# A GEGLU block with Strassen products: T3 of the second half from DRAM, and M2 of one group next to M1 of the next

## The chip, the cores and the metric

The kernel runs on 1 core of one Trainium2 chip. The metric is device time in microseconds (us), the median of several executions. Before the change it is 539.02 us (three runs, 538.69 to 539.37).

## The reference

```python
"x": (1, 2048, 1024), "w_gate": (1024, 3584), "w_up": (1024, 3584), "w_down": (3584, 1024)  # bf16

def reference(x, w_gate, w_up, w_down):
    return (_gelu(x @ w_gate) * (x @ w_up)) @ w_down     # _gelu: tanh form
```

## The kernel before

The 2048 rows are worked through in two halves (h = 0, 1) of 1024. Each half has two stages. The first computes the hidden values hT = gelu(x @ w_gate) * (x @ w_up), 3584 features by 1024 rows, in bf16 (matmuls at lines 267 and 418). The second, "down", multiplies by w_down in two groups (grp = 0, 1) of 512 rows, one call of `down_group` each (matmuls at line 698). Both stages use a Strassen-Winograd scheme: seven products of half-size blocks in place of eight.

In a down group the blocks are A11, A12, A21, A22 of hT and B11, B12, B21, B22 of w_down. A product has 14 blocks of the contraction (NS = 14) and two row tiles (u = 0, 1), so 28 matmuls of 128x128 by 128x512. M1 = A11 B11 and M2 = A12 B21 read bf16 operands directly. The other five read sums in f32: M5 = S1 T1, M6 = S2 T2, M7 = S3 T3, M3 = S4 B22, M4 = A22 T4. The order is M1, M5, M6, M7, M2, M3, M4. The partial results stay in eight PSUM banks, in four pairs PB, VB, QB, RB: ACT copies M1 from PB to QB, M6 adds to QB, ACT copies that to RB, M7 adds to RB, and so on; M2 adds to PB and closes the first output block.

**The ring of right operands.** T1, T2, T3, B22 (as f32) and T4 of a group, 14 blocks each, pass through a ring `t_mem` of NR = 20 blocks (`right`, line 567). A block's place is its number in that sequence modulo 20. A new pair of blocks can be written when the pair 20 places earlier has been used. `t_down` (line 587) makes one pair: T1 and T3 by a subtraction on DVE (line 600), B22 by a cast on ACT (line 597), T2 and T4 by a 512 KB load from `t_dram` (line 595), where the first stage of h = 0 put them (`stage_step`, line 614, store at line 627). The functions `behind_m5`, `behind_m6`, `behind_m7`, `behind_m3`, `behind_m4` are called after each second block of a product and issue what can go where the used blocks were: T2 and the first of T3 behind M5, T3 behind M6, B22 and the first three pairs of T4 behind M7, the other four pairs of T4 behind M3, the next group's T1 and T2 behind M3 and M4. The left sums S1 to S4 are made on DVE (`s_down`, line 670), A22 is cast on ACT (line 662). The first four blocks of S3 of group one lie in a weight buffer, `early`.

**B21** is loaded by `load_b21` (line 555) behind M6's fifth and sixth block: three tiles of 512 KB from a pool of three buffers (`wd_pool`) and a fourth of 256 KB from the output pool (`o_pool`, four buffers). In group one one of the three buffers is `early`, so the third load waits until M7 has read it.

**Order.** Every engine's queue is fixed by hand: `sp`, `act`, `dve`, `pool` and `pe` chain each instruction behind the last one of its engine, in program order. All loads and stores of the down stage are on SP's one queue. `product` (line 692) takes an order of the matmuls: `plain` goes block by block, both u; `tail` finishes u = 0 five matmuls before the end; `head` begins with five of u = 0.

In group one of h = 0, after M6, `x_fill` (line 997) loads 1 MB of the next half's x from DRAM on SP (line 1000).

Of the kernel before, what the change touches and what calls it, by code (L numbers as in the profile page):

```python
# [11 lines left out]
F32 = mybir.dt.float32  # L12
# [22 lines left out]
def kernel(  # L35
# [8 lines left out]
    nc = tc.nc  # L44
    P = 128
# [8 lines left out]
    NH = 2  # L54
# [4 lines left out]
    DN = 512  # L59
# [9 lines left out]
    NS = KF // 2  # L69
    NR = 20  # L70
    NGRP = SH // TB
# [15 lines left out]
    dram_pool = ctx.enter_context(  # L87
        tc.tile_pool(name="dram", bufs=1, space=bass.MemoryType.DRAM)
    )
# [10 lines left out]
    w_mem = shared_pool.tile([P, 4 * CH + (NS - 4) * DN], BF16, name="w_mem")  # L100
    assert NR * DN == 5 * KH * TB and NS - 4 >= 2 * KD // 2

    t_dram = dram_pool.tile([P, NS, 2, DN], F32, name="t_dram")
    x_dram = dram_pool.tile([KD, P, TB], BF16, name="x_dram")

    banks = [psum.tile([P, TB], F32, name=f"bank{i}") for i in range(8)]
    PB, VB, QB, RB = (0, 1), (2, 3), (4, 5), (6, 7)
    last_on = {}

    def on(engine, inst):  # L110

        if engine in last_on:
            tc.add_manual_dep(
                inst.ins, last_on[engine].ins.name, SCHED_DEP, reason="engine order"
            )
        last_on[engine] = inst
        return inst

    def sp(inst):
        return on("sp", inst)  # L120

    def act(inst):
        return on("act", inst)

    def dve(inst):
        return on("dve", inst)
# [12 lines left out]
    def pe(inst):  # L139
        return on("pe", inst)  # L140
# [391 lines left out]
    def wd_rows(i0, i1):  # L532

        assert i1 <= 8 or i0 >= 8
        e0 = 2 * CH + i0 * D if i1 <= 8 else (i0 - 8) * D
        return w_mem[:, e0 : e0 + (i1 - i0) * D].rearrange("p (a b) -> p a b", b=D)

    def b22_blocks(i0, i1):

        assert i1 <= 4 or i0 >= 4  # L540
        e0 = (NS - 8) * D + i0 * DN if i1 <= 4 else 4 * CH + (i0 - 4) * DN
        return w_mem[:, e0 : e0 + (i1 - i0) * DN].rearrange("p (a b) -> p a b", b=DN)
# [7 lines left out]


    BPT = WDT * D // DN
    b21_tiles = {}

    def load_b21(n, q):
        i0, i1 = q * BPT, min((q + 1) * BPT, NS)
        if i1 < NS:
            w = wd_pool.tile([P, WDT, D], BF16, name="wd_sb")
            w = w[:].rearrange("p a d -> p (a d)")
        else:  # L560
            w = o_pool.tile([P, (i1 - i0) * DN], BF16, name="o_sb")[:]
        w = w.rearrange("p (b n) -> p b n", n=DN)
        src = wdv[:, NS + i0 : NS + i1, 0:DN]
        sp(nc.sync.dma_start(out=w[:, 0 : i1 - i0, :], in_=src))
        b21_tiles[(n, q)] = w

    def right(grp, name, i0, i1):

        r0 = ((grp * len(SEQ) + SEQ.index(name)) * NS + i0) % NR
        assert r0 + i1 - i0 <= NR  # L570
        t = t_mem[:, r0 * DN : (r0 + i1 - i0) * DN]
        return t.rearrange("p (a b) -> p a b", b=DN)
# [14 lines left out]
    def t_down(grp, name, i0, i1):  # L587

        for i in range(i0, i1, 2):
            t = right(grp, name, i, i + 2)  # L590
            rows = wd_rows(i, i + 2)
            b11, b12 = rows[:, :, 0:DN], rows[:, :, DN:D]
            if name in ("t2", "t4"):
                src = t_dram[:, i : i + 2, 0 if name == "t2" else 1, :]
                sp(nc.sync.dma_start(out=t.bitcast(F32), in_=src))
            elif name == "b22":
                act(nc.scalar.copy(out=t, in_=b22_blocks(i, i + 2)))  # L597
            else:
                in0, in1 = (b12, b11) if name == "t1" else (b22_blocks(i, i + 2), b12)
                dve(nc.vector.tensor_tensor(out=t, in0=in0, in1=in1, op=ALU.subtract))  # L600

    staged = {}
# [68 lines left out]
    NSPLIT = 4  # L673
    DH = DN // 2

    def down_group(hT, h, grp, then):
        last_grp = h == NH - 1 and grp == NGRP - 1
        more = grp + 1 < NGRP
        t0 = grp * TB
        n = h * NGRP + grp  # L680

        def done(name):
            for f in then.get(name, ()):
                f()

        plain = [(i, u) for i in range(NS) for u in range(2)]
        tail = [p for p in plain if p[0] < NS - 5]
        tail += [(i, u) for u in range(2) for i in range(NS - 5, NS)]
        head = [(i, u) for u in range(2) for i in range(5)]
        head += [p for p in plain if p[0] >= 5]  # L690

        def product(name, bset, lhs, rhs, start, stop, behind=None, order=plain):

            left_of = [0] * NS
            for i, u, *part in order:
                bank, c0, c1 = part or (bset[u], 0, DN)
                pe(
                    nc.tensor.matmul(  # L698
                        banks[bank][:, c0:c1],
                        lhsT=lhs(i, u),  # L700
                        rhs=rhs(i)[:, c0:c1],
                        start=start and i == 0,
                        stop=stop and i == NS - 1,
                        skip_group_check=True,
                    )
                )
                left_of[i] += 1
                if behind is not None and left_of[i] == 2 and i % 2 == 1:
                    behind(i - 1)

        def h_block(l, j):
            def lhs(i, u):
                c0 = t0 + (2 * l + u) * P
                return hT[:, j * NS + i, c0 : c0 + P]

            return lhs
# [15 lines left out]
        def b21(i):  # L732
            return b21_tiles[(h * NGRP + grp, i // BPT)][:, i % BPT, :]

        def add_m5(dst, src, u):
            dve(
                nc.vector.tensor_tensor(
                    out=banks[dst][:], in0=banks[src][:], in1=m5[u][:], op=ALU.add
                )
            )  # L740

        def evacuate(bset, l, d, halves=False):

            outs = []
            for u in range(2):
                if halves and u == 1:
                    r0 = h * SH + t0 + (2 * l + u) * P
                    for bank, c in ((bset[u], 0), (VB[u], DH)):
                        dst = o_pool.tile([P, DN], BF16, name="o_sb")[:, 0:DH]
                        src = banks[bank][:, c : c + DH]  # L750
                        if c == 0:
                            dve(nc.vector.tensor_copy(out=dst, in_=src))
                        else:
                            act(nc.scalar.copy(out=dst, in_=src))  # L754
                        c0 = d * DN + c
                        outs.append((out2[r0 : r0 + P, c0 : c0 + DH], dst))
                    continue
                dst = o_pool.tile([P, DN], BF16, name="o_sb")[:]
                r0 = h * SH + t0 + (2 * l + u) * P
                if last_grp and u == 0:  # L760
                    dve(nc.vector.tensor_copy(out=dst, in_=banks[bset[u]][:]))
                else:
                    act(nc.scalar.copy(out=dst, in_=banks[bset[u]][:]))  # L763
                outs.append((out2[r0 : r0 + P, d * DN : (d + 1) * DN], dst))
            return outs

        def store(outs):
            for dst, src in outs:
                sp(nc.sync.dma_start(out=dst, in_=src))
# [1 line left out]
        def store_last(dst, src):  # L771
            act(nc.scalar.dma_start(out=dst, in_=src))

        product("m1", PB, h_block(0, 0), b11, True, False)
        for u in range(2):
            act(nc.scalar.copy(out=banks[QB[u]][:], in_=banks[PB[u]][:]))
        done("m1")

        def behind_m5(i):

            s_down(hT, grp, "s2", i, i + 2)
            if NT2 + i < NS:
                t_down(grp, "t2", NT2 + i, NT2 + i + 2)
            elif more:
                late.append(i + NT2 - NS)
            else:
                t_down(grp, "t3", i + NT2 - NS, i + NT2 - NS + 2)
# [12 lines left out]
        def behind_m6(i):  # L800
            if NT2 + i < NS:
                t_down(grp, "t3", NT2 + i, NT2 + i + 2)
            else:
                s_down(hT, grp, "s4", i + NT2 - NS, i + NT2 - NS + 2)
            if i == 4:
                for q in range(4):
                    load_b21(n, q)

        product("m6", QB, lsum(0), rsum("t2"), False, False, behind_m6, tail)
# [1 line left out]
        for u in range(2):  # L811
            act(nc.scalar.copy(out=banks[RB[u]][:], in_=banks[QB[u]][:]))
            add_m5(QB[u], QB[u], u)
        t_down(grp, "b22", 0, NT2)
        done("m6")

# [9 lines left out]
        s_down(hT, grp, "a22", 0, NS)  # L826
        out22 = evacuate(VB, 1, 1)
        done("m7")
        store(out22)
        product("m2", PB, h_block(0, 1), b21, False, True)  # L830
        out11 = evacuate(PB, 0, 0)
        done("m2")


# [6 lines left out]
                    t_down(grp + 1, "t1", NT2 + i - NS, NT2 + i - NS + 2)  # L841

        product("m3", QB, lsum(0), rsum("b22"), False, True, behind_m3)
        store(out11 + evacuate(QB, 0, 1))
        done("m3")

        def behind_m4(i):
            if not more:
# [28 lines left out]
    for h in range(NH):  # L877
# [52 lines left out]
        for lead in range(begin, NPAIR, PPG):  # L930
# [15 lines left out]
            for n, pair in enumerate(members):  # L946
# [7 lines left out]
                if h > 0 and 6 < pair < 11:  # L954
                    i = s3_late[pair - 7]
# [112 lines left out]
```

## Time and profile before

| | |
|---|---|
| median of 3 runs | 539.02 us |
| the profiled execution | 539.16 us |
| its span, first to last instruction | 537.4 us |
| PE (matmul) busy | 533.6 us, 99% |
| DVE, ACT, POOL busy | 367.6, 263.5, 252.2 us |
| DMA, mean over the span | 191 GB/s |
| down stage of h = 0 | 183.0 to 270.9 us |
| down stage of h = 1 | 446.5 to 534.4 us |

Engines: PE is the matmul engine, PEld its weight loads, DVE the vector engine, ACT the scalar engine, POOL GpSimd, SP the queue of SyncE (SPq where it issues a DMA). L595 is line 595 of the kernel. A line of a timeline has the start in us, the length in us, the engine, the line, the operation, what it writes and reads, the number of instructions merged into it and, in brackets, the idle time before it and what ended it. For a DMA on SPq the length is that of the issue; the time to landing is asked for separately. A matmul's recorded length (0.38 to 0.39 us) overlaps the next one's; the distance of the starts is its cost. A line of the chain has start, length, what. A line of a table by stretches has the stretch, its length, each engine's busy time with its number of instructions, the granted PE clock, the DMA engines' share and GB/s. Waits read: who, what it waited for, us in total, times, longest.

### The profile page before, as it was taken

What the parts mean: (1) busy time and instruction counts of PE and PEld (TensorE: products, weight loads), DVE (VectorE), ACT (ScalarE), POOL (GpSimd) and SP (SyncE); (2) the same over time, 40 slices, a digit from 0 to 9 for tenths busy, and PEclk for the clock granted to TensorE, in tenths of its full rate; (3) what the DMA queues carried; (4) which work ended last, traced back from release to release, by engine and by line L of the source; (5) the groups of instructions that cost most, each with busy time, mean ns of one, the idle gap of its engine ahead of it and who ended that gap; (6) DMA issues with size and microseconds to landing.
All of it is one profiled execution on the core that took longest, in us unless ns stands there. A gap on an engine that the chain in (4) does not pass through costs nothing.

```text
span 537.4 us, 7033 instructions
## 1 busy us (share of the span) xinstructions
PE 533.6 (99%) x2388; PEld 379.2 (71%) x2388; DVE 367.6 (68%) x476; ACT 263.5 (49%) x447; POOL 252.2 (47%) x213
## 2 busy tenths in 40 slices
PE   9999999999999999999999999999999999999997
PEld 4568686867677686777768676776768686866866
DVE  2985868787876998989555353444444669979961
ACT  2555555556465329117465554656555551452280
POOL 0698696969696200000056494958677670000000
PEclk9999999999999999999999999999999999999999
DMA  9965759697623887788950413314040329677846
GB/s 220 329 199 134 267 164 304 182 320 199 229 53 143 318 288 243 243 292 292 329 168 12 145 62 97 110 48 154 3 156 22 136 84 337 228 237 250 292 143 212
DMA packets 92547, 102.70 MB, mean 191 GB/s; under 512 B 18656, under 2 KB 67424, under 8 KB 92512
## 3 DMA queue, kind: packets, MB, share of 16 engines
q1 hardware_dynamic: 69568, 80.23, 45.7%
q10 hardware_dynamic: 22944, 22.02, 13.2%
q8 instruction: 19, 0.31, 0.3%
q14 instruction: 16, 0.13, 0.1%
HBM read 85.98 MB, written 12.58 MB: 183 GB/s over the span
## 4 chain that ended last, share of the span: by engine, by line
PE 99%; ACT 0%; issue 0%
PE bank L418 63%; PE bank L698 33%; PE bank L267 3%; PE bank L202 1%; PE bank L311 0%; ACT o_sb L754 0%
## 5 line engine op out<-in xcount | busy, mean ns | idle before, releaser
L418 PE MATMUL bank<-t_mem,s_mem 128*128 128x512 f32 x1056 | 244.6, 392 | 0.0
L418 PEld LDWEIGHTS bank<-t_mem,s_mem 128*128 128x128 f32 x1056 | 198.1, 188 | 42.7 <-issue 0.2
L388 POOL TENSOR_TENSOR s_mem<-w_mem 128x512 fp32r<-128x512 bf16 x102 | 124.0, 1236 | 185.5 <-DMA out_dram<-o_sb 96.9
L698 PE MATMUL bank<-t_mem,s_mem 128*128 128x512 f32 (+1 forms) x548 | 127.2, 391 | 0.0
L698 PEld LDWEIGHTS bank<-t_mem,s_mem 128*128 128x128 f32 x548 | 102.5, 188 | 22.0
L291 DVE TENSOR_TENSOR hT<-w_mem,bank 128x512 bf16<-128x512 f32 x106 | 72.5, 687 | 66.5 <-PE bank L418 44.5
L434 DVE TENSOR_TENSOR bank<-bank,m 128x512 f32<-128x512 f32 x108 | 70.0, 694 | 56.1 <-ACT m L472 54.3
L418 PE MATMUL bank<-xT,w_mem 128*128 128x512 bf16 x432 | 95.7, 379 | 0.0
L286 ACT ACTIVATE w_mem<-bank 128x512 f32<-128x512 f32 x106 | 63.0, 597 | 64.1 <-DVE bank L434 34.8
L418 PEld LDWEIGHTS <-w_mem 128*128 128x128 bf16 x432 | 41.2, 98 | 51.3 <-issue 3.4
L388 POOL TENSOR_TENSOR s_mem<-w_mem,s_mem 128x512 fp32r<-128x512 bf16 x52 | 68.4, 1335 | 2.9 <-PE bank L418 2.9
L600 DVE TENSOR_TENSOR t_mem<-w_mem 128x1024 fp32r<-128x1024 bf16 x56 | 65.9, 1225 | 0.9 <-PE bank L418 0.9
L388 POOL TENSOR_TENSOR s_mem<-s_mem,w_mem 128x512 fp32r<-128x512 f32 x52 | 61.3, 1200 | 0.0
L401 ACT CAST s_mem<-w_mem 128x512 fp32r<-128x512 bf16 x54 | 33.2, 616 | 31.3 <-PE bank L418 30.1
L478 ACT COPY bank<-bank 128x512 f32<-128x512 f32 x54 | 30.8, 570 | 26.6 <-PE bank L418 26.6
L670 DVE TENSOR_TENSOR s_mem<-hT 128x512 fp32r<-128x512 bf16 x52 | 36.7, 745 | 7.1 <-PE bank L698 7.1
L472 ACT COPY m<-bank 128x512 f32<-128x512 f32 x54 | 31.8, 589 | 18.4 <-PE bank L418 18.4
L698 PEld LDWEIGHTS <-hT 128*128 128x128 bf16 x224 | 21.3, 98 | 26.6 <-issue 2.1
L444 ACT COPY bank<-bank 128x512 f32<-128x512 f32 x54 | 30.7, 570 | 14.3 <-PE bank L418 13.5
L625 DVE TENSOR_TENSOR o_sb<-wd_sb,o_sb 128x512 fp32r<-128x512 bf16 x28 | 32.9, 1176 | 0.5
L763 ACT CAST o_sb<-bank 128x512 bf16<-128x512 f32 x27 | 14.8, 585 | 33.8 <-PE bank L698 33.8
L597 ACT CAST t_mem<-w_mem 128x1024 fp32r<-128x1024 bf16 x28 | 26.9, 1047 | 0.0
(46 smaller groups left out, 236.5 us busy)
## 6 DMA issues: line engine op xcount, KB each, us to landing
t_mem<-t_dram SPq DMA_DIRECT2D x56, 512.0 KB, 5.3
w_mem<-in_w_gate_dram ACTq DMA_DIRECT2D x10, 1024.0 KB, 5.4
w_mem<-in_w_up_dram ACTq DMA_DIRECT2D x10, 1024.0 KB, 8.3
wd_sb<-in_w_down_dram SPq DMA_DIRECT2D x28, 256.0 KB, 5.4
t_dram<-o_sb SPq DMA_DIRECT2D x28, 256.0 KB, 3.5
wd_sb<-in_w_down_dram SPq DMA_DIRECT2D x12, 512.0 KB, 7.6
w_mem<-in_w_down_dram SPq DMA_DIRECT2D x4, 1024.0 KB, 6.7
w_mem<-in_w_down_dram SPq DMA_DIRECT2D x8, 512.0 KB, 8.3
```

Of the source, the lines that this page charges most:

```text
L286: act(nc.scalar.activation(out=g_sb, in_=ps[:], func=ACT.Gelu_apprx_tanh))
L291: nc.vector.tensor_tensor(out=hT[:, fc, tb * TB : (tb + 1) * TB], in0=g_sb, in1=ps[:], op=ALU.mult,)
L388: pool(nc.gpsimd.tensor_tensor(out=t, in0=in0, in1=in1, op=op))
L401: act(nc.scalar.copy(out=t, in_=a(1, 1)))
L418: nc.tensor.matmul(banks[bank][:], lhsT=lhs[:, c, :], rhs=rhs[:, c, :], start=start and c == 0, stop=c == KH - 1, skip_group_check=True,)
L434: nc.vector.tensor_tensor(out=banks[dst][:], in0=banks[src][:], in1=m5[:], op=ALU.add)
L472: act(nc.scalar.copy(out=m5[j][:], in_=banks[V_[j]][:]))
L478: act(nc.scalar.copy(out=banks[R_[j]][:], in_=banks[Q_[j]][:]))
L600: dve(nc.vector.tensor_tensor(out=t, in0=in0, in1=in1, op=ALU.subtract))
L625: dve(nc.vector.tensor_tensor(out=t, in0=in0, in1=in1, op=ALU.subtract))
L670: dve(nc.vector.tensor_tensor(out=t, in0=in0, in1=in1, op=op))
L698: nc.tensor.matmul(banks[bank][:, c0:c1], lhsT=lhs(i, u), rhs=rhs(i)[:, c0:c1], start=start and i == 0, stop=stop and i == NS - 1, skip_gr ...
```

## The change

`t_dram` gets a third plane. In group one of h = 0, T3 is still made on DVE; the new `keep_t3`, behind M6, issues seven 512 KB stores of it on SP. In group two of h = 0, T3 is made on DVE as before. In h = 1 (`one_run`) both groups load T3 from there, seven 512 KB loads each, at the places where the subtractions were issued.

In h = 1, M2 leaves its place between M7 and M3. M2 of group one is held and goes in front of group two's M1; group two's M2 follows right behind its M1 (M1 in order `tail`, M2 in order `head`). So the second half runs M1 M5 M6 M7 M3 M4 | M2 M1 M2 | M5 M6 M7 M3 M4. The last group swaps the bank pairs PB and VB. The first three tiles of B21 are loaded once for both groups, behind group one's M6, the fourth twice. In h = 0 the products keep their order.

```diff
-    t_dram = dram_pool.tile([P, NS, 2, DN], F32, name="t_dram")
+    t_dram = dram_pool.tile([P, NS, 3, DN], F32, name="t_dram")
@@ load_b21
+        if i1 < NS and n == NH * NGRP - NGRP:
+            b21_tiles[(n + 1, q)] = w
@@ t_down
-            if name in ("t2", "t4"):
-                src = t_dram[:, i : i + 2, 0 if name == "t2" else 1, :]
+            if name in ("t2", "t4") or (name == "t3" and t3_from_dram):
+                src = t_dram[:, i : i + 2, ("t2", "t4", "t3").index(name), :]
                 sp(nc.sync.dma_start(out=t.bitcast(F32), in_=src))
...
                 dve(nc.vector.tensor_tensor(out=t, in0=in0, in1=in1, op=ALU.subtract))
+                if name == "t3" and not t3_kept:
+                    t3_new.append((t_dram[:, i : i + 2, 2, :], t.bitcast(F32)))
+    def keep_t3():
+        for dst, src in t3_new:
+            sp(nc.sync.dma_start(out=dst, in_=src))
+        t3_kept.extend(t3_new)
+        t3_new.clear()
@@ down_group
+        one_run = h == NH - 1
+        if one_run:
+            t3_from_dram.append(grp)
+        last_grp = one_run and grp == NGRP - 1
+        PB, VB = ((2, 3), (0, 1)) if last_grp else ((0, 1), (2, 3))
...
-        product("m1", PB, h_block(0, 0), b11, True, False)
+        def m2(order=plain):
+            product("m2", PB, h_block(0, 1), b21, False, True, None, order)
+            return evacuate(PB, 0, 0)
+        if held:
+            store(held.pop()())
+        m1_order = tail if last_grp else plain
+        product("m1", PB, h_block(0, 0), b11, True, False, None, m1_order)
         for u in range(2):
             act(nc.scalar.copy(out=banks[QB[u]][:], in_=banks[PB[u]][:]))
         done("m1")
+        if last_grp:
+            load_b21(n, NQ21 - 1)
+            store(m2(head))
@@ behind_m6
-            if i == 4:
-                for q in range(4):
+            if i == 4 and not last_grp:
+                for q in range(NQ21 - 1 if one_run else NQ21):
                     load_b21(n, q)
@@ after m6
+        keep_t3()
         t_down(grp, "b22", 0, NT2)
         done("m6")
@@ after m7
-        store(out22)
-        product("m2", PB, h_block(0, 1), b21, False, True)
-        out11 = evacuate(PB, 0, 0)
+        if not one_run:
+            store(out22)
+            out22 = m2()
@@ after m3
-        store(out11 + evacuate(QB, 0, 1))
+        store(out22 + evacuate(QB, 0, 1))
         done("m3")
+        if one_run and more:
+            load_b21(n, NQ21 - 1)
+            held.append(m2)
```

More of the change, by code (lines that the diff above doesn't have):

```diff
@@ L552 @@
     BPT = WDT * D // DN
+    NQ21 = -(-NS // BPT)
     b21_tiles = {}
@@ L600, in t_down @@
                 dve(nc.vector.tensor_tensor(out=t, in0=in0, in1=in1, op=ALU.subtract))
+                if name == "t3" and not t3_kept:
+                    t3_new.append((t_dram[:, i : i + 2, 2, :], t.bitcast(F32)))
+    t3_new = []
+    t3_kept = []
+    t3_from_dram = []
+    def keep_t3():
[3 more added lines that the diff above has]
+        t3_new.clear()
     staged = {}
@@ L674 @@
     DH = DN // 2
+    held = []
     def down_group(hT, h, grp, then):
-        last_grp = h == NH - 1 and grp == NGRP - 1
+        one_run = h == NH - 1
[3 more added lines that the diff above has]
+        PB, VB = ((2, 3), (0, 1)) if last_grp else ((0, 1), (2, 3))
         more = grp + 1 < NGRP
```

## The prediction, made before the changed kernel ran

> **What bounds the kernel now.** I read the chain of waits in order of time first, then the waits of the matmul engine (PE), then PE's and SyncE's (SP's) timelines around one group of each half's down stage, then single landings.
>
> ```profile
> by line: PE bank L418 63.0%; PE bank L698 32.7%; PE bank L267 2.7%; PE bank L202 0.6%; PE bank L311 0.2%; ACT o_sb L754 0.1%; issue 0.0%
> ...
> 0.77 3.15 PE bank L202 x7
> ...
> 6.87 12.95 PE bank L267 x60
> ...
> 183.03 87.89 PE bank L698 x392
> 270.92 175.56 PE bank L418 x784
> 446.48 87.95 PE bank L698 x396
> ```
>
> The chain is matmuls from end to end; the two down stages (L698) are 87.9 us each. The waits of PE are one line, at the start:
>
> ```profile
> PE bank L202 <- PEq L1052: 0.8, 1, 0.8
> ```
>
> So no wait on an engine or a DMA can be taken from PE. What is left is its rate. PE's timeline of the second half's first group shows it:
>
> ```profile
> 452.19 13.09 PE L698 MATMUL bank<-t_mem,s_mem 128*128 128x512 f32 x56
> 465.12 1.07 PE L698 MATMUL bank<-t_mem,wd_sb 128*128 128x512 f32 x4
> ...
> 471.47 5.35 PE L698 MATMUL bank<-wd_sb,hT 128*128 128x512 bf16 x24
> 476.66 1.03 PE L698 MATMUL bank<-o_sb,hT 128*128 128x512 bf16 x4
> ```
>
> M5 and M6 are 56 f32 matmuls from 452.19 to M7's start at 465.12; inside such a run the starts lie 227 ns apart, those of bf16 216 ns. A product of 28 is 6.35 us in f32, 6.05 us in bf16. M7 starts at 465.12, M2 at 471.47.
>
> The other side is SP's queue. It works in program order, so a waiting load holds all behind it. In the first half's first group:
>
> ```profile
> 203.90 0.37 SPq L564 DMA_DIRECT2D wd_sb<-in_w_down_dram  x1
> 204.31 0.51 SPq L564 DMA_DIRECT2D o_sb<-in_w_down_dram  x1
> 204.86 1.02 SPq L1000 DMA_DIRECT2D xT<-x_dram  x2
> 206.39 2.31 SPq L595 DMA_DIRECT2D t_mem<-t_dram  x3
> 213.22 0.83 SPq L769 DMA_DIRECT2D out_dram<-o_sb  x2
> 215.19 3.10 SPq L595 DMA_DIRECT2D t_mem<-t_dram  x4
> ```
>
> The third b21 load (L564, 203.90) had waited for M7's first matmuls to free its buffer; then come b21's rest, x's two loads, three T4 loads, two stores, four T4 loads. In the second half's first group the same load waits until 467.35:
>
> ```profile
> 453.50 0.36 SPq L595 DMA_DIRECT2D t_mem<-t_dram  x1
> ...
> 456.24 0.36 SPq L595 DMA_DIRECT2D t_mem<-t_dram  x1
> 456.65 1.30 SPq L564 DMA_DIRECT2D wd_sb<-in_w_down_dram  x2
> 467.35 0.37 SPq L564 DMA_DIRECT2D wd_sb<-in_w_down_dram  x1
> ```
>
> **The price of one 512 KB transfer.** Fast end: in a stretch with a full queue the busy times by engine, the clock, the DMA share and, last, the GB/s were
>
> ```profile
> 447.00:453.00 6.00, 6.00 (x29) 3.03 (x28) 6.00 (x8) 0.64 (x2) 0.00 (x0) 1.00 1.06 378
> ```
>
> 378 GB/s, so 524288 bytes take 1.39 us. Slow end: the last T4 load of the first group, issued at 217.94, was asked for its landing:
>
> ```profile
> DMA to landing us min/median/max: 6.1/6.1/6.1
> ```
>
> It landed at 224.0; the third b21 load (203.90, 3.6 us to landing) at 207.5. Between them a never empty queue moved 256 KB + 2x512 + 7x512 + 2x128 KB, ten times 512 KB: 16.5 us, 1.65 us each. I take 1.5, midway, for reads and writes alike: the 128 KB stores of this kernel land 0.34 us apart when they follow each other, 1.36 us per 512 KB. [...]
>
> **1. Seven stores of T3 (first half, first group).** `keep_t3` stands behind all of M6's code, so on SP behind the b21 loads, which are held until M7 has begun, and in front of x's loads and T4's. Each store costs SP some 0.33 us (the stores of L627), 2.3 us in all, hidden behind the transfers. The transfers are not hidden: the queue was full from 204 to 224, so T4's last pair lands 7 x 1.5 = 10.5 us later. M4 takes its last pair seven matmuls before its end; M1 of the next group follows at 226.81, so the pair is needed at 226.81 - 7 x 0.227 = 225.2. It landed at 224.0, 1.2 us early. Stall: 10.5 - 1.2 = **9.3 us** (8.5 at 1.39; 10.4 at 1.65). The stores also hold ring slots that ACT's b22 casts overwrite: the last of those waits for the fourth store, 209.1 (b21's end) + 4 x 1.5 = 215.1, plus 1.05 for the cast; M3 wants it at 219.5, so 3.3 us cover it. ACT's a22 casts (3.73 us) and the out22 copies queue behind and end near 221; SP's stores of out22 wait for these, T4's last four loads behind them, issued by about 224, while the queue is full until 227. No bubble.
>
> **2. T3 by DMA, second half, first group.** DVE loses seven subtractions of 1.2 us per group; PE waited for none, so the gain is 0. On SP seven loads come in: three behind M5's, three in M6, then b21's three, and the seventh T3 pair behind these. From the last T2 load, which landed at 456.24 + 6.0 = 462.2, the queue has six T3 pairs, three b21, one T3 pair: 462.2 + 10 x 1.5 = 477.2. The third b21 is issued near 467.4 as before, when about six are still queued, so its wait makes no hole. M7 wants the last pair as its 25th matmul, 465.12 + 24 x 0.227 = 470.6. Stall **6.7 us** (5.5 to 8.1).
>
> **3. The same, last group.** No b21 loads here. T2's last landed at 500.19 + 6.1 = 506.3; seven T3 pairs behind it end at 506.3 + 10.5 = 516.8. M7 started 6.35 before M2 (515.41), at 509.06, and wants the last pair at 514.5. Stall **2.3 us** (1.5 to 3.4).
>
> **4. M2 moved.** Four bf16 blocks become two in the second half. From the last f32 start before M2 (471.24) to the twelfth f32 start after it (480.06) are 8.83 us, where 28 x 0.216 + 12 x 0.227 is 8.77: a change of type and back costs 0.06 us. Gain **0.12 us**. M2 right behind M1 needs ACT's copy of the first bank within five bf16 matmuls, 1.08 us; M6 to M7 does the same in 1.13 us, with the copy (0.57 us) done 0.3 us early, so 0. Its b21 is there; three loads saved in the last group stood on nobody's path. What M2's place covered, 6 us for T4 behind M7, is gone: from T3's last landing to M4's last pair are then 0.9 + 6.35 + 5.0 = 12.2 us for at most seven loads, 10.5 us (11.6 at 1.65): the next thing to be late, by 0 here.
>
> **5. The clock after a long wait.** In step 2 PE stands still for over 5 us at a stretch, in step 1 for some 4 before M4's first pair. No idle PE of that length is in this trace. The nearest row is the start: seven matmuls in 3.15 us, 427 ns apart, and this until 5.8, though the granted clock reads 1.00: 5 us at half speed, 2.5 us lost. Bounds 0 and 2.5 per long stall; I take **1.5** once (step 1's is mostly hidden by the wait for the next pair). [...]
>
> **Sum.** 9.3 + 6.7 + 2.3 + 1.5 - 0.1 = 19.7 us. The profiled execution took 539.16 us (span 537.4 and 1.8 around it), the median is 539.02; the sum goes on the median: **558.7 us**. Ends: 8.5 + 5.5 + 1.5 - 0.1 = 15.4, so 554.4; 10.4 + 8.1 + 3.4 + 5.0 = 26.9, so 565.9.
>
> **Rivals.** (a) Only one place bites: the stores stall M4, but in the second half the backlog runs off faster than my mean, or T3's seventh pair gets past b21; or the reverse. Without step 1 it is 549, without steps 2, 3 and 5 it is 548: 548 to 549. For it: holes in the queue stood near its beginnings, and a long backlog has fewer. Against: even 1.39 us leaves 5.5 us. (b) Not slower, 538.9: the extra 11 MB vanish in gaps. The point at which it decides is 1.2/7 = 0.17 us per store and 8.4/10 = 0.84 us per transfer in step 2; no row is under 1.3. (c) Faster: the switches would have to cost nine times what the rows show to give 1.1 us. (d) Both long stalls halve the clock, T4 becomes late too: 567 to 572.
>
> **How the numbers follow.** Forecast 0.78, (a) 0.12, (b) 0.04, (c) 0.01, (d) 0.05. A measurement of this kernel tells 0.2%, 1.1 us. Faster 0.01, same 0.04, slower 0.95. The range runs from (a)'s lower end, 548, to the edge of (d), 567, and leaves out (b), (c) and most of (d).
>
> **What would show it.** Right: PE waits appear on DMA t_mem<-t_dram at L698: in the first half's first group some 9 us in M4, in the second half some 7 us late in M7 of the first group, 2 us in the second; DVE at L600 falls by 14; t_dram gets seven 512 KB stores near 205 to 220; 427 ns spacing behind the longest wait. Wrong: M4 of the first group starts without a wait (stores cost nothing), T3's seventh load issued ahead of the third b21, or PE waits at M3 for the b22 casts or at M4 for T4 in the second half.

## The result and the profile after

The changed kernel takes 558.19 us, the median of five runs (556.58 to 559.92), against 539.02 us before (538.69 to 539.48): a ratio of 1.0355, interval 1.0328 to 1.0382. The forecast was 558.7 us, with a range of 548 to 567. The profiled execution is the longest of the five: 559.92 us, span 558.1 us, 20.7 us more than the span before.

PE's waits were one line at the start. Now they read (who, for what, us in total, times, longest):

```profile
PE bank L718 <- DMA t_mem<-t_dram: 10.0, 7, 4.9
PE bank L418 <- DVE hT L291: 2.1, 1, 2.1
PE bank L202 <- PEq L1086: 0.8, 1, 0.8
PE bank L718 <- DVE s_mem L684: 0.3, 1, 0.3
```

L718 is the down stage's matmul (L698 before). Ten us of waits are for loads from `t_dram`; the 0.3 us put down to DVE ends with a T3 load too, which landed at 477.1. The second line, a wait of the first stage for DVE, was not foreseen.

Laying the starts of the stages beside those of before gives where the span went:

| | before | after, first profile | after, second profile (e10) |
|---|---|---|---|
| first stage, h = 0 | 182.1 | 186.1 | 181.7 |
| down stage, h = 0 | 87.9 | 94.6 | 94.9 |
| first stage, h = 1 | 175.6 | 175.6 | 175.6 |
| down stage, h = 1 | 88.1 | 98.0 | 100.2 |
| span | 537.4 | 558.1 | 556.1 |

The 3.7 to 3.8 us that the four stages leave are the time ahead of the first matmul and behind the last.

**The first half's down stage.** SP's timeline after, to be held against the six lines of before:

```profile
207.92 0.37 SPq L565 DMA_DIRECT2D wd_sb<-in_w_down_dram  x1
208.34 0.51 SPq L565 DMA_DIRECT2D o_sb<-in_w_down_dram  x1
208.94 7.41 SPq L613 DMA_DIRECT2D t_dram<-t_mem  x7
216.40 2.83 SPq L1034 DMA_DIRECT2D xT<-x_dram  x2
219.70 3.40 SPq L598 DMA_DIRECT2D t_mem<-t_dram  x3
223.63 0.83 SPq L789 DMA_DIRECT2D out_dram<-o_sb  x2
224.50 3.04 SPq L598 DMA_DIRECT2D t_mem<-t_dram  x4
```

The seven stores (L613) stand where they were expected, in front of x's loads and all of T4. The last T4 load, issued at 227.19, took 8.5 us to land, at 235.7; M4, which needs it, was due to begin at 224.5. PE's timeline shows M4 starved pair by pair:

```profile
227.26 5.79 PE L718 MATMUL bank<-t_mem,s_mem 128*128 128x512 f32 x16 [2.61 <-DMA t_mem<-t_dram]
233.24 0.94 PE L718 MATMUL bank<-t_mem,s_mem 128*128 128x512 f32 x3 [0.19 <-DMA t_mem<-t_dram]
234.59 0.70 PE L718 MATMUL bank<-t_mem,s_mem 128*128 128x512 f32 x2 [0.41 <-DMA t_mem<-t_dram]
235.87 1.85 PE L718 MATMUL bank<-t_mem,s_mem 128*128 128x512 f32 x7 [0.58 <-DMA t_mem<-t_dram]
```

The last line is the pair that seven matmuls were to follow: x7, to the end of M4.

**The second half's down stage.** SP's queue in group one, and PE's M7:

```profile
470.64 2.17 SPq L598 DMA_DIRECT2D t_mem<-t_dram  x3
472.87 6.14 SPq L565 DMA_DIRECT2D wd_sb<-in_w_down_dram  x3
479.06 2.47 SPq L598 DMA_DIRECT2D t_mem<-t_dram  x2
```

```profile
478.45 3.96 PE L718 MATMUL bank<-t_mem,s_mem 128*128 128x512 f32 x15
487.31 4.94 PE L718 MATMUL bank<-t_mem,s_mem 128*128 128x512 f32 x14 [4.90 <-DMA t_mem<-t_dram]
```

T3's seventh load is issued at 479.06, behind three B21 loads, and takes 8.2 us; PE goes on at 487.31, when it has landed. Afterwards 14 matmuls take 4.94 us where 15 took 3.96.

**The clock.** A table by stretches (length, busy time and instructions of PE, PEld, DVE, ACT, POOL, granted clock, DMA share, GB/s) shows why:

```profile
162.80:166.20 3.40, 3.40 (x9) 1.22 (x9) 3.40 (x6) 0.57 (x1) 0.00 (x0) 0.50 0.90 247
227.70:231.10 3.40, 3.40 (x10) 2.49 (x9) 2.10 (x3) 0.73 (x2) 0.00 (x0) 0.50 1.06 399
487.10:490.50 3.40, 3.19 (x8) 2.52 (x9) 1.30 (x2) 1.08 (x3) 0.00 (x0) 0.50 0.34 120
166.50:170.00 3.50, 3.50 (x17) 2.14 (x16) 1.38 (x2) 1.06 (x3) 0.00 (x0) 1.00 1.00 387
```

At the end of each of the three long waits the granted clock is 0.50 for 3.4 us; then it is 1.00 again (the fourth line).

### The profile page after: what moved, and what is told of

Read it like the earlier page. It is cut to its first block, busy times and chain, and to the rows that moved or that the text cites. A ratio compares the mean times of both kernels' runs of the same rounds, so it can differ in the third digit from the quotient of the medians.

```text
span 558.1 us, 7031 instructions
## 1 busy us (share of the span) xinstructions
PE 540.5 (97%) x2366; PEld 380.8 (68%) x2388; DVE 354.8 (64%) x462; ACT 263.9 (47%) x447; POOL 251.3 (45%) x213
## 3 DMA queue, kind: packets, MB, share of 16 engines
q10 hardware_dynamic: 22944, 22.02, 12.8%
## 4 chain that ended last, share of the span: by engine, by line
PE 91%; DMA 6%; issue 1%; DVE 1%; SPq 0%; ACT 0%; DVEq 0%
PE bank L418 60%; PE bank L718 28%; DMA t_mem<-t_dram 6%; PE bank L267 3%; PE bank L202 1%; PE bank L311 0%; DVE hT L291 0%; DVE s_mem L684 0%; DVE o_sb L639 0%; ACT o_sb L774 0%; SPq L565 0%; DVEq L684 0%; DVEq L291 0%; SPq L598 0%
## 5 line engine op out<-in xcount | busy, mean ns | idle before, releaser
L718 PE MATMUL bank<-t_mem,s_mem 128*128 128x512 f32 (+1 forms) x548 | 132.4, 399 | 10.5 <-DMA t_mem<-t_dram 10.0
L718 PEld LDWEIGHTS bank<-t_mem,s_mem 128*128 128x128 f32 x548 | 103.7, 192 | 37.4 <-DMA t_mem<-t_dram 8.6
L388 POOL TENSOR_TENSOR s_mem<-w_mem,s_mem 128x512 fp32r<-128x512 bf16 x52 | 66.7, 1303 | 3.3 <-PE bank L418 3.3
L603 DVE TENSOR_TENSOR t_mem<-w_mem 128x1024 fp32r<-128x1024 bf16 x42 | 49.8, 1226 | 2.2 <-PE bank L718 1.3
L718 PEld LDWEIGHTS <-hT 128*128 128x128 bf16 x224 | 21.4, 98 | 26.6 <-issue 1.6
L684 DVE TENSOR_TENSOR s_mem<-hT 128x512 fp32r<-128x512 bf16 x52 | 34.5, 701 | 5.2 <-PE bank L718 5.2
L639 DVE TENSOR_TENSOR o_sb<-wd_sb,o_sb 128x512 fp32r<-128x512 bf16 x28 | 36.7, 1310 | 0.5
```

Of the source, the lines that this page charges most:

```text
L388: pool(nc.gpsimd.tensor_tensor(out=t, in0=in0, in1=in1, op=op))
L684: dve(nc.vector.tensor_tensor(out=t, in0=in0, in1=in1, op=op))
L718: nc.tensor.matmul(banks[bank][:, c0:c1], lhsT=lhs(i, u), rhs=rhs(i)[:, c0:c1], start=start and i == 0, stop=stop and i == NS - 1, skip_gr ...
```

## The experiments

All ratios and times stand beside runs of the kernel before on the same chip.

**e1: the third plane alone.**

```diff
-    t_dram = dram_pool.tile([P, NS, 2, DN], F32, name="t_dram")
+    t_dram = dram_pool.tile([P, NS, 3, DN], F32, name="t_dram")
```

> The kernel before with one line changed: t_dram has its third plane, which nothing uses. Theory A (the stall of 4.0 us that the changed kernel's profile shows in the first stage of the first half, where one DVE subtraction takes 5.1 us beside a busy GpSimd, is a race between these two engines, tipped by stores that land late): no fixed cost of the layout, 539 us, at most some executions up to 4 us longer. Rival B (the wider rows of t_dram make the first stage's stores slower each time): 541 to 543 us in every execution.

539.36 us against 539.73, ratio 0.9999 (0.9979 to 1.0019); the kernel before ran from 538.57 to 541.29 there. No cost of the layout shows; B falls.

**e2: the stores alone.** The second half as before.

```diff
-        one_run = h == NH - 1
-        if one_run:
-            t3_from_dram.append(grp)
+        one_run = False
...
```

> The changed kernel's first half with the seven stores of T3, the second half as before (T3 on DVE, M2 in its old place). Theory A (the stores delay T4's loads on SP's queue): M4 of the first half's first group waits as in the changed kernel, so that down stage takes 94.6 us (before 87.9), the second half's 87.9; 545.8 us, up to 4 more where the first stage stalls. Rival B (the wait in M4 belongs to something else in the change): the first half's down stage 87.9 us, 539 us.

547.15 us, ratio 1.0142 (1.012 to 1.0165). Down stages in its profile: 94.9 us in the first half, 88.1 in the second. PE's new waits, but for 0.2 us at the start, are M4's:

```profile
PE bank L716 <- DMA t_mem<-t_dram: 3.5, 2, 2.9
```

The first half's excess belongs to the stores, all of it.

**e4: the loads alone.**

```diff
-                src = t_dram[:, i : i + 2, ("t2", "t4", "t3").index(name), :]
+                src = t_dram[:, i : i + 2, ("t2", "t4", "t3").index(name) % 2, :]
...
-        keep_t3()
...
```

> The changed kernel without the seven stores; the loads of T3 in the second half read T2's plane instead, so T3's values are left out of the computation, the transfers are the same. Theory A (the second half's stalls come from its own loads alone): the first half's down stage 87.9 us, the second's 97.8 us as in the changed kernel; 548.9 us, up to 4 more where the first stage stalls. Rival B (the stores of the first half leave something behind, in the queue or in DRAM, that slows the second half): second half under 95 us.

552.51 us, ratio 1.0245 (1.0216 to 1.0275). The first half's down stage 87.9 us, the second's 99.9, between the 98.0 and 100.2 of the changed kernel's two profiles; A's 97.8 and 548.9 were too low. PE's new waits are all in that stage:

```profile
PE bank L716 <- DMA t_mem<-t_dram: 6.6, 5, 4.7
```

The halves are separate; B falls.

**e3: M2 moved, T3 on DVE.**

```diff
-        if one_run:
-            t3_from_dram.append(grp)
...
-        keep_t3()
...
```

> M2 moved in the second half as in the change, T3 on DVE everywhere, no stores, two planes. Theory A (M2's old place covers DVE, which makes T3, then S4, then adds M5 to the banks of M3): without it M3 of group one waits for DVE some 3 us (in the profile before, DVE is done with that addition at 474.8, M7 ends at 471.5) and of group two some 1 us; 542 to 543 us. Rival B (DVE is in time, and only two changes of type are saved): 538.9 us.

545.44 us, ratio 1.0095 (1.0062 to 1.0127); its runs spread from 542.78 to 546.47. The second down stage takes 92.15 us, 4.06 more; the first stage of its profile has 3.1 us more too (below), which A's 542 to 543 us did not count. PE, then DVE, at the start of group one's M3:

```profile
477.40 2.81 PE L714 MATMUL bank<-t_mem,s_mem 128*128 128x512 f32 x10 [2.71 <-DVE bank L753]
```

```profile
473.56 3.09 DVE L682 TENSOR_TENSOR s_mem<-hT,s_mem 128x512 fp32r<-128x512 bf16 x5
476.56 2.48 DVE L753 TENSOR_TENSOR bank<-bank,m 128x512 f32<-128x512 f32 x4
```

M3's bank is ready only when DVE, behind S4 (L682), has added M5 to it (L753). So M2's old place did cover DVE, and T3 from DRAM is what buys the move. The move itself saves what was priced: the spacings of M3 that are longer than 0.227 us add up to 4.15 us, the stage is 4.06 us longer; 0.1 us is left for the two changes of type.

**e5: B21 behind T4.**

```diff
-            if i == 4 and not last_grp:
-                for q in range(NQ21 - 1 if one_run else NQ21):
+            if i == 4 and not one_run:
+                for q in range(NQ21):
                     load_b21(n, q)
...
+            if i == 6 and one_run and more:      # behind_m3
+                for q in range(NQ21 - 1):
+                    load_b21(n, q)
```

> The changed kernel, with the three big B21 loads of the second half moved from behind M6 to behind M3, after T4's last load. Theory A (group one's M7 waits because three B21 loads stand between T3's sixth and seventh pair): the seventh pair lands one transfer behind the sixth, the 5.3 us wait falls to 1 to 2 us and the half clock behind it goes; second half's down stage 92.3 us (98.0 in the changed kernel), 552.5 us. Rival B (T3's loads are late by themselves, whatever stands between): over 95 us, no less than 556 us.

551.13 us, ratio 1.0223 (1.0209 to 1.0237); second down stage 93.3 us. M7 of group one, from its tenth matmul, runs into M3 with no idle time over 0.15 us:

```profile
474.92 9.35 PE L718 MATMUL bank<-t_mem,s_mem 128*128 128x512 f32 x35
```

The seventh pair landed at 479.4, 1.3 us behind the sixth. The 4.9 us wait was the B21 loads between T3's sixth and seventh pair, as A has it; the stage stays 1.0 us over A's 92.3, and the last group's M7 now loses 2.9 us instead of 2.3.

**e6: x's load out of the way, and e13: T4 without its wait.**

```diff
-            then0["m6"] = [x_fill]
+            then0["m4"] = [x_fill]
```

> The changed kernel, with the 1 MB load of the next half's x in the first half's group one moved from behind M6 to behind M4. Theory A (M4 waits for as many bytes as stand in front of T4 on SP's queue): two transfers of 1.5 us fewer, the first half's down stage 91.6 us (94.6 in the changed kernel), 555.2 us. Rival B (T4's loads wait for the stores' completion to free their ring places, not for bytes): 94 us or more, 558 us.

557.71 us, ratio 1.0338 (1.0307 to 1.0368); the first down stage 94.3 us. Two transfers less in front of T4, and only 0.3 to 0.6 us gained on the changed kernel's two profiles: A failed as written, and B's numbers came. SP's timeline shows T4's first three loads spread out:

```profile
216.01 3.57 SPq L598 DMA_DIRECT2D t_mem<-t_dram  x3
220.00 0.83 SPq L789 DMA_DIRECT2D out_dram<-o_sb  x2
220.88 2.59 SPq L598 DMA_DIRECT2D t_mem<-t_dram  x4
```

Each of the three waits for the store that frees its ring place: they were issued at 216.01, 218.01 and 219.22, when the fifth, sixth and seventh store had just landed (215.96, 217.95, 219.14). They themselves landed at 220.4, 222.9 and 225.0, 2.3 us apart: x's loads had only filled that gap. e13 takes the wait away on top of it, by two edits that it does not tell apart:

```diff
-        for dst, src in t3_new:
+        for dst, src in t3_new[4:] + t3_new[:4]:
...
-            store(out22)
-            out22 = m2()
+            out22 = out22 + m2()
...
-        store(out22 + evacuate(QB, 0, 1))
+        store(out22)
+        store(evacuate(QB, 0, 1))
```

> The changed kernel with x's load behind M4, T3's last three pairs stored first (T4's first three pairs need their ring places), and the first half's out22 stores behind T4's loads. Theory A (with x's load out of the way T4's loads came too thinly, because each waits for a store's completion, and the queue ran with holes of 1 us; without that wait T4 follows the stores without a hole): first half's down stage 91.5 us (94.3 with x's load moved alone). Rival B (the stores' bytes cost more than their time in the queue, T4's loads run slower behind them): 94 us or more.

556.09 us, ratio 1.0315 (1.0298 to 1.0332); first down stage 92.9 us, of which 1.1 us is a new wait in group two (for DVE, L603). The seven T4 loads now follow the stores in one run:

```profile
209.61 2.55 SPq L613 DMA_DIRECT2D t_dram<-t_mem  x2
212.27 6.34 SPq L598 DMA_DIRECT2D t_mem<-t_dram  x7
```

They land 1.29 to 1.76 us apart. The result lies between A's 91.5 and B's 94; without the new wait it would be 91.8. So the stores delay T4 in two ways, by their bytes in the queue and by the ring places that they hold. With x's loads in between, the second adds nothing; without them it costs about what x's bytes had cost (94.3 against 91.8).

**e12: a smaller dose.**

```diff
-            if name in ("t2", "t4") or (name == "t3" and t3_from_dram):
+            if name in ("t2", "t4") or (name == "t3" and t3_from_dram and i >= NT2):
...
-                if name == "t3" and not t3_kept:
+                if name == "t3" and not t3_kept and i >= NT2:
```

> A smaller dose: only T3's last four pairs of seven are stored and loaded, the first three are made on DVE in every group. Theory A (each store and load is one transfer of 1.36 to 1.5 us in front of what PE waits for): four stores instead of seven, first half's down stage 90.5 us (94.6 in the changed kernel); in the second half seven transfers instead of ten between T2's last pair and T3's last, so 1.9 us in group one's M7, none in group two's, 89.9 us (98.0); 543.4 us. Rival B (a fixed cost of the detour, not the bytes): first half above 93, second above 95 us.

548.39 us, ratio 1.0175 (1.016 to 1.019). First down stage 91.2 us: 3.3 above before for four stores, 6.8 for seven, so 1.1 to 1.2 us for each of the three left out. The second, 93.2 us, is worse than A's 89.9: the seven transfers from T2's last to T3's last took 11.5 us (466.4 to 477.9), 1.64 each against 1.5 for the ten of the changed kernel, and PE stood for 3.3 us at a stretch. The mean granted clock of its profile is 0.997, that of the kernel before 1.000.

**e9: the three moves together.** e5, e6 and the DVE step of e8.

> The changed kernel with all three moves: B21 late, x late, the DVE step away from GpSimd. Theory A (the three causes are separate and add up): first half's down stage 91.6, second's 92.3 us, no stall in the first stage; 546.8 us. Rival B (what is taken away in one place comes back in another, T4 or M2 late): above 550 us.

549.71 us, ratio 1.0196 (1.0182 to 1.021); down stages 93.3 and 93.4 us. The time is just under B's 550, and far over A's 546.8. It is 1.4 us better than e5 alone; in its profile the clock stays at 1.00, and no wait is over 1 us. The first stage has no stall (182.3 us). The x move brings less than A asked, as e6 says.

**The first stage.** In the first profile of the changed kernel a DVE subtraction that makes T4 (L639) takes 5.12 us beside GpSimd (POOL):

```profile
156.94 5.12 DVE L639 TENSOR_TENSOR o_sb<-wd_sb,o_sb 128x512 fp32r<-128x512 bf16 x1
```

```profile
157.00 2.28 POOL L388 TENSOR_TENSOR s_mem<-w_mem 128x512 fp32r<-128x512 bf16 x2
159.23 2.28 POOL L388 TENSOR_TENSOR s_mem<-w_mem,s_mem 128x512 fp32r<-128x512 bf16 x2
```

It ends at 162.06, 0.55 us after the last of POOL's four instructions. Before, the same step took 1.47 us and POOL's were the longer ones, two in 2.73 and two in 3.17 us:

```profile
156.85 1.47 DVE L625 TENSOR_TENSOR o_sb<-wd_sb,o_sb 128x512 fp32r<-128x512 bf16 x1
```

PE waits 2.1 us behind it, then runs at a granted clock of 0.50 for 3.4 us; the stage is 4.0 us longer than before. e3, which changes nothing there, had such a step at another place (4.85 us at 57.5); PE waited 1.8 us behind it, and the mean granted clock of that profile is 1.00. Three runs asked what that does to the median. e10 is the changed kernel again, unedited; e8 and e11 move one of the steps to where POOL rests, in the kernel before and in the changed one (other steps still run beside POOL, one of them at 148.5 in e8's profile, for 1.43 us):

```diff
-                add(0, "m1", lambda n=3 if few else 4: run_steps(n))
+                add(0, "m1", lambda n=3 if few else 5: run_steps(n))
...
-                    add(n, "m3", lambda: run_steps(1), run_loads)
+                    if n == 0 or few:
+                        add(n, "m3", lambda: run_steps(1))
+                    add(n, "m3", run_loads)
```

> The changed kernel itself, once more, for a second profile. Theory A (the 4.0 us in the first stage of its first profile, one DVE step held by GpSimd and the half clock behind it, is a chance that some executions take): first stage near 182 us in this profile, down stages near 94.6 and 98 us, 555.5 to 556.5 us; or again a stall elsewhere in the first stage. Rival B (the change brings it each time): again near 186 us.

> The kernel before; in the first half's first stage one of the nine DVE steps of each two pairs that make T2 and T4 is moved from behind M3 of the second pair, where GpSimd is busy, to behind M1, where it rests. Theory A (the stalls of 3 to 4 us in some executions of the first stage come from such a step held by GpSimd): the long executions go, all within 538.5 to 539.3, median 538.8 and below the kernel before on the same chip. Rival B (they come from elsewhere, the start or the DMA): the same spread as the kernel before, 538.6 to 541.5.

> The changed kernel with one DVE step of each two pairs of the first stage moved from behind M3 to behind M1, where GpSimd rests. Theory A (the stall comes from such a step, in some executions): median 1.5 to 2.5 us under the changed kernel's on the same chip and a spread of under 1.5 us. Rival B (the spread of the changed kernel comes from its second half's loads): no difference.

e10: 557.77 us (556.89 to 557.92), and its profile has no stall in the first stage, 181.7 us. Of the eleven profiles of the changed kernel and its variants (the first, and e2 to e13 without e8) only the first and e3's have it: the stall is a chance, not something that the change brings each time. What takes its place there is a longer wait in group one's M7:

```profile
PE bank L718 <- DMA t_mem<-t_dram: 11.6, 7, 6.1
```

6.1 us instead of 4.9, with the clock at 0.50 for 6.8 us instead of 3.4:

```profile
482.40:489.20 6.80, 4.89 (x12) 3.82 (x13) 1.99 (x3) 1.59 (x3) 0.00 (x0) 0.50 0.53 182
```

e8: 539.22 against 539.05 us, ratio 1.0003 (0.9994 to 1.0012); the kernel before had no long execution on that chip, so nothing follows. e11: 557.54 against e10's 557.77, spread 556.15 to 559.87: no difference, as B has it. That the spread comes from the second half's loads, B's reason, is not shown: there is one profile to a run, and the two of the changed kernel differ by 4.4 us in the first stage and by 2.2 in the last. How often the first stage stalls stays open.

No version beats the kernel before, and the runs point to none: PE has no wait there, and all that the change can save is 0.1 us.

## Why the prediction was right

**The stores (9.3 us; measured 6.8 and 7.0).** Mechanism right, size some 2.4 us too high, below the lower end of 8.5. The stores themselves were near: from B21's end (208.34 + 4.8 = 213.1) to the last store's landing (215.08 + 7.6 = 222.7) are 9.5 us, 1.36 each, not 1.5. The step that failed is the rest: x's loads, T4's and the two out stores behind them took 13.1 us (222.66 to 235.74), where before the same work took 14.9. The price of 1.5 was the mean of a row with holes and one without, added onto a queue whose own holes were already in its landing time; a longer queue closed 1.8 us of them. 9.5 - 1.8 - 1.2 = 6.5; the 0.2 to 0.3 us left lie between the last landing and M4's end, where the seven matmuls began 0.13 us late and took 0.11 us longer. That a long backlog has fewer holes stood in the first rival, as an argument for it; it belonged in the sum. The prediction also named the ring places that the stores hold for the b22 casts alone; T4's first three loads wait for them too (e6). In the changed kernel that cost nothing: behind x's loads they landed 1.28 to 1.36 us apart. The b22 casts, ACT's row and out22 cost PE nothing, as worked out.

**T3's loads in group one (6.7 us).** Right. T2's last landed at 467.02 + 5.3 = 472.3, T3's last at 487.3: ten transfers in 15.0 us, 1.5 each. M7 began at 475.89 and wanted the pair at 481.3: 6.0 us. The third B21 load, issued late at 478.64, made no hole, as worked out: it landed 1.5 us behind the second, and T3's last pair 1.4 us behind it. e5 shows that the three B21 loads were the cause. In e4 and e10 the same ten came later still, so the term is 6 to 7.

**The last group (2.3 us).** The longer spacings of M7 add up to 2.3 us.

**M2's move (-0.12 us).** e3 has it at 0.1, as the difference of two sums of 4 us. T4 in the second half, named as the next to be late, was not.

**The clock (1.5 us, once).** The halving came at the end of both long waits, as the profile's 0.50 shows. In group one it cost 1.6 us in the first profile and 2.4 in e10, where it held for 6.8 us; in M4 it cost nothing, since the last load, landing at 235.74, set M4's end. The 1.00 that the prediction read for the kernel's first 5.8 us is no reading: the clock's records of that trace begin at 5.89. In the first profile the clock read 0.50 for 3.41 us each time. A wait of 2.1 us was followed by it at 162.8, while one of 2.7 us in e3 was not. The last section has more of these waits.

**The sum (19.7 us; measured 20.7 in the first profile's span, 18.7 in the second's, 19.2 between the medians).** In the first profile the stores are 2.5 us under their term, the second half 0.5 under, and the first stage has 4.0 that the sum lacked; in the second profile the stores are 2.3 under, the first stage 0.4 under and the second half 1.7 over its 10.4. So misses of both signs hid each other, and the 0.5 us between forecast and median is better than the working was: that closeness is luck.

The first rival, one place only, falls with e2 and e4: each place alone costs, by the medians beside each other, 7.4 and 12.8 us. (b) would have needed transfers of under 0.84 us each; the loads from `t_dram` in the trace after land 1.26 us apart or more (one store came 0.84 us behind another, which had itself come 2.20 us behind the one before). (c) would have needed changes of type that cost 1.1 us; e3 leaves 0.1. Of (d) one part came: the clock was halved behind both long waits, but T4 of the second half was not late.

## What to carry to other kernels

An operand that an engine made while PE waited for nothing was not cheaper to load here: seven 512 KB stores in SP's in-order queue made the first down stage 7.0 us longer (e2), the loads and the move the second one 11.8 (e4). So list what stands in the queue between the new transfer and the next thing that PE wants, and subtract that thing's slack, which here was 1.2 us. Price a transfer that joins a full queue by the full queue's rate (here 1.36 us for 512 KB), and one that joins a thin queue by the landing times there (2.3 us apart in e6), and do not mix the two. Look at the granted clock behind PE's waits: here it read 0.50 for 3.4 us at the end of waits of 2.1, 2.6 and 4.9 us in the first profile, and stayed at 1.00 in e9, where no wait was over 1 us.

## What the runs showed of the hardware that was not expected

- The granted clock fell to 0.50 behind some of PE's waits and not behind others. In the first profile after it read 0.50 from 162.80, 227.65 and 487.07, for 3.41 us each time, with waits of 2.06, 2.61 and 4.90 us that ended at 162.71, 227.26 and 487.31. In e10 it held for 6.8 us, with a wait of 6.1. In e6 it read 0.50 behind two waits of 1.1 and 1.0 us (the first two rows below; PE is busy for 1.27 us of the first). In e3 it stayed at 1.00 through a wait of 2.7 us (the last two rows). So the length of a wait alone did not tell whether the clock would fall; what decides it is not shown.

```profile
221.80:225.10 3.30, 1.27 (x5) 0.67 (x4) 3.30 (x4) 0.00 (x0) 0.00 (x0) 1.00 1.00 340
225.20:228.50 3.30, 3.30 (x7) 2.22 (x8) 2.81 (x3) 1.07 (x2) 0.00 (x0) 0.50 1.03 367
```

```profile
472.60:476.00 3.40, 2.08 (x10) 1.39 (x8) 3.40 (x7) 3.40 (x5) 0.00 (x0) 1.00 0.74 220
476.10:479.40 3.30, 1.97 (x8) 1.45 (x9) 3.30 (x6) 3.30 (x8) 0.00 (x0) 1.00 0.85 290
```

- A DVE subtraction of two SBUF operands took 5.1 us while GpSimd ran four subtractions back to back, and 1.47 us in the kernel before at the same place. GpSimd's four took 2.28 us for each two in the first case, 2.73 and 3.17 in the second. Why DVE was slow in the one and not in the other is not shown.
- Stores to DRAM of 512 KB passed at 1.36 us each on average, as the loads did in a full queue (1.32 to 1.37 us for the second to sixth of T3's in group one); loads that were issued one at a time, each behind the landing of a store, landed up to 2.5 us apart (e6).
